# Two-layer decode block on one core: output projection in 512-column products, row quarters summed by an fp32 product, w_down in two loads

## The chip, the core and the metric

One NeuronCore of a Trainium2 chip runs the whole kernel. Its engines each take their own instructions in order: TensorE (PE; its weight loads are shown as PEld), VectorE (DVE), ScalarE (ACT), GpSimd (POOL) and SyncE (SP), which here issues nearly all transfers. Engines wait for one another through semaphores. The metric is the device time of one execution in microseconds, as the median of several runs; a profiled execution gives the trace.

## The reference

Four sequences decode one token each through attention, a gated feed-forward network, the same attention again and the same network again:

```python
x = x + A(_layernorm(x), k_cache, v_cache, wq, wo)
x = x + B(_layernorm(x), w_gate, w_up, w_down)
x = x + A(_layernorm(x), k_cache, v_cache, wq, wo)
x = x + B(_layernorm(x), w_gate, w_up, w_down)

def A(x, k_cache, v_cache, wq, wo):      # B=4, D=512, 32 query heads, 8 kv heads, 4096 keys, head size 128
    q = (x @ wq) as 32 heads; each kv head serves 4 query heads
    p = softmax(q @ k.T * 128 ** -0.5)
    return (p @ v, all 32 heads side by side: 4096 values) @ wo

def B(x, w_gate, w_up, w_down):          # F = 1792
    return (gelu(x @ w_gate) * (x @ w_up)) @ w_down
```

All inputs are bf16. Both layers use the same caches and weights. K and V of one sequence and one kv head are 1 MB each.

## The kernel before

**Staging.** The weights are loaded once and stay: `wq` (4 MB), `wo` in two halves of 2 MB, `wg`, `wu` and `wd` (1.75 MB each). K and V go through `KV`, a tile of 12 slots of 1 MB. The K of a batch element stays in its eight slots for both layers. The V of heads 0 to 6 is loaded a second time for the second layer, that of head 7 is held. So few slots are left to rotate, and a load into a slot waits until the last product that reads it is done. For the last batch element the tile of `wq`, which has no reader any more, gives four more slots. Every load is one instruction on SP's queue (`ld_head` L293, `plain` L650, `ld_wo` L685); SP waits there for the slot, and all later loads wait behind.

**The order of the work.** `Plan` holds every step as a node with an engine, an assumed duration, the steps that it needs, and for TensorE a number of instructions (`ins`). `Plan.run` is a list scheduler: it walks a simulated clock and picks, per engine, the next ready node, with a model of the transfers (`DMA_KB` us per KB and others) and of the fetching of TensorE's instructions in blocks (`BLOCK`, `FIRST_BLOCK`, `FETCH`). Its order is then emitted as it stands, for every engine. The constants thus change only the order. Where it foresees TensorE idle, `spin` (L888) puts in filler matmuls on the identity, whose results nothing reads.

**One batch element `b`, layer `L`.** K heads 5 and 7 are transposed on TensorE (`kturn` L306) and copied back by ACT (`kcopy` L312); the others by DVE in two halves (`turn` L299, node `tn`). Scores of four heads at a time are 32 matmuls (`scores` L348, nodes `sc`), each z in two halves m; then the maximum, the exponent (ACT L371), a transposition on DVE and TensorE (`pswap` L388, in the PSUM tiles T0 and T1; copied by ACT L396), the sums (L401) and the V products: one node `val` per head, 32 matmuls of 128x128 weights (`values` L417). `oscale` (L425, nodes `os`) divides and writes the heads' columns into `OT`.

**The output projection.** `proj` (L547) multiplies each query head's column of `OT` by its 128 rows of `wo`, in four matmuls of 128 columns, each into its own 32-row quarter of the PSUM tile `R0`. The quarter t thus holds output columns 128t to 128t+127. In the first layer the heads are done in three groups as they become ready, `groups` giving (0,1,2,3), (4,5,6), (7); in the second layer all four sequences are projected together at the end of the kernel (`op2`), in four groups. `addback` (L555, L556) transposes the quarters and adds them to `XT`. Then follow the norm (`ln`: L432, L438, L444, L445, L454, ACT L461 and L462), gate and up products (`up` L564), the turn (L571), the GELU in pieces (L587 to L616), `down` (L624, 56 matmuls of 128 columns), `addback` again, the norm and, in the first layer, the query product of the second (`qproj`: L470, ACT L483, DVE L488) and its spreading (`spread_q`: `qs` L527, the replicating product `qp` L537, `qx` L325) ahead of the second layer's scores. The K slots of batch element b are free only after these scores, and so they gate the K loads of b+1. The first V products of the second layer are put between these steps.

**The end.** After the last V load: the remaining V products, `op2`, `addback`, norm, up, GELU, `down`, and the output row (L636, L637, L641), written out by four small transfers (L644).

## Time and profile before

Median of three runs 302.95 us (302.27 to 304.44).

| | |
|---|---|
| profiled execution | 302.36 us |
| its span, first to last instruction | 300.5 us |
| mean granted TensorE clock | 0.949 |
| PE busy | 227.4 us (76%), 4705 matmuls |
| PEld busy | 145.4 us (48%) |
| DVE busy | 132.1 us (44%) |
| ACT busy | 70.0 us (23%) |
| read from HBM | 110.37 MB, 367 GB/s over the span |
| V products L417 | 1920 matmuls on KV, 64.6 us busy |
| projection L547 | 640 matmuls, 14.2 us busy |
| fillers L888 | 181 matmuls |

Busy times of the engines overlap, and a matmul counts as busy for its whole passage through the pipeline, so the 227 us of PE are no measure of what TensorE would need. The idle time of an engine costs only where others wait for it. The chain of waits follows the work that ended last back to what released it; the waits of SP's queue say what each load stood for; "issue" is idle time of an engine in which the profile shows nothing that it waited for.

### The profile page before, as it was taken

The numbers are of one execution on the slowest core, as the hardware profiler recorded it, in microseconds if no ns is written. First come the engines' busy times: TensorE is split into PE (matmuls) and PEld (weight loads), VectorE is DVE, ScalarE is ACT, GpSimd is POOL, SyncE is SP. The second block draws the span as 40 slices with busy tenths as digits, with TensorE's granted clock in tenths as the row PEclk, the third lists the DMA queues.
The fourth block names the chain that finished last, engine by engine and source line by source line (L and its number), as shares of the span: only waits on it lengthen the run. The fifth ranks groups of instructions, "written<-read, shape, count | busy, mean of one in ns | idle before, by whom it ended". The sixth has DMA issues, their size and how long they took to land.

```text
span 300.5 us, 10242 instructions
## 1 busy us (share of the span) xinstructions
PE 227.4 (76%) x4705; PEld 145.4 (48%) x4705; DVE 132.1 (44%) x374; ACT 70.0 (23%) x157; POOL 0.7 (0%) x6
## 2 busy tenths in 40 slices
PE   5987657766778898786868996777577858699694
PEld 1432435432333576554434676553336646457562
DVE  4187702002488642143388730342888205243024
ACT  1020921000021671001215730010247300122000
POOL 0000000000000000000000000000000000000000
PEclk9999999999999799799797997997999999799869
DMA  8999999999949999999999999999999999999600
GB/s 310 409 422 420 366 415 417 399 392 426 416 171 424 421 418 417 416 380 382 366 387 426 418 417 398 373 382 354 374 425 420 413 377 388 368 373 429 266 4 1
DMA packets 18059, 111.02 MB, mean 369 GB/s; under 512 B 1633, under 2 KB 5729, under 8 KB 5729
## 3 DMA queue, kind: packets, MB, share of 16 engines
q1 hardware_dynamic: 17968, 110.37, 91.7%
q8 instruction: 36, 0.59, 0.8%
q14 instruction: 7, 0.05, 0.1%
q10 hardware_dynamic: 48, 0.01, 0.0%
HBM read 110.37 MB, written 0.00 MB: 367 GB/s over the span
## 4 chain that ended last, share of the span: by engine, by line
DMA 53%; PE 24%; SPq 10%; DVE 6%; issue 4%; ACT 3%; DVEq 0%
DMA KV<-in_A_v_cache_dram 34%; DMA KV<-in_A_k_cache_dram 12%; PE O_ps L417 10%; SPq L293 7%; PE S_ps L348 6%; DMA wd_sb<-in_B_w_down_dram 6%; PE R_ps L547 3%; SPq L650 3%; PE R_ps L306 2%; PE R_ps L470 1%; ACT KV L312 1%; DVE KV L299 1%; ACT PA L396 1%; PE R_ps L624 1%; PE T_ps L388 1%
## 5 line engine op out<-in xcount | busy, mean ns | idle before, releaser
L417 PE MATMUL O_ps<-PA,KV 128*128 128x56 bf16 x1920 | 64.6, 191 | 28.6 <-DMA KV<-in_A_v_cache_dram 19.6
L417 PEld LDWEIGHTS <-KV 128*128 128x128 bf16 x1920 | 58.8, 98 | 42.7 <-DMA KV<-in_A_v_cache_dram 30.0
L299 DVE STREAM_TRANSPOSE KV<-KV 128x1024 int32<-128x1024 int32 x48 | 57.0, 1218 | 3.4 <-DMA KV<-in_A_k_cache_dram 3.4
L888 PE MATMUL S_ps<-iden_b 128*128 128x512 bf16 x161 | 42.6, 393 | 3.6 <-DVE iden_b L266 3.6
L348 PE MATMUL S_ps<-KV,PA 128*32 128x512 bf16 x384 | 39.3, 442 | 7.1 <-DVE rdk L407 3.6
L312 ACT ACTIVATE KV<-R_ps 128x512 bf16<-128x512 f32 x64 | 35.1, 596 | 36.2 <-PE R_ps L306 36.2
L888 PEld LDWEIGHTS <-iden_b 128*128 128x128 bf16 x181 | 17.2, 105 | 25.4 <-issue 8.4
L306 PE MATMUL R_ps<-iden_b,KV 128*128 128x128 bf16 x256 | 23.1, 225 | 7.3 <-DMA KV<-in_A_k_cache_dram 3.8
L461 ACT ACTIVATE sm<-sm 128x1 f32<-128x1 f32 (+1 forms) x10 | 2.0, 204 | 102.9 <-DVE sm L454 102.9
L354 DVE TENSOR_REDUCE sm<-S_ps 128x1 f32<-128x512 f32 x16 | 10.8, 674 | 32.6 <-PE S_ps L348 32.6
L306 PEld LDWEIGHTS <-KV 128*128 128x128 bf16 x256 | 16.4, 101 | 15.9 <-issue 8.8
L348 PEld LDWEIGHTS <-PA 128*32 128x32 bf16 x384 | 12.8, 102 | 19.0 <-DVE PA L325 7.2
L547 PE MATMUL R_ps<-wo_sb,OT 128*1 128x128 bf16 (+1 forms) x640 | 14.2, 250 | 5.4 <-DMA wo_sb<-in_A_wo_dram 2.2
L371 ACT ACTIVATE PA<-S_ps,sm 128x512 bf16<-128x512 f32 x16 | 11.7, 732 | 25.9 <-DVE sm L365 11.2
L348 PE MATMUL S_ps<-KV,QN 128*32 128x512 bf16 x128 | 16.4, 381 | 0.0
L547 PEld LDWEIGHTS <-OT 128*1 128x1 bf16 (+1 forms) x640 | 11.4, 96 | 7.8 <-issue 4.3
L425 DVE TENSOR_TENSOR OT<-O_ps,XS 128x12 bf16<-128x12 f32 (+1 forms) x8 | 1.3, 167 | 30.8 <-PE O_ps L417 30.8
L425 DVE TENSOR_TENSOR OT<-O_ps,rdk 128x16 bf16<-128x16 f32 (+3 forms) x17 | 2.9, 170 | 23.4 <-PE O_ps L417 23.3
L470 PE MATMUL R_ps<-wq_sb,xn 128*1 128x512 bf16 (+1 forms) x160 | 11.1, 417 | 1.9 <-DVE xn L445 1.9
L396 ACT ACTIVATE PA<-T_ps 128x512 bf16<-128x512 f32 x16 | 9.5, 595 | 11.1 <-PE T_ps L388 11.1
L571 DVE STREAM_TRANSPOSE PA<-R_ps 128x448 f32<-128x448 f32 x10 | 6.5, 649 | 12.2 <-PE R_ps L564 12.2
L380 DVE STREAM_TRANSPOSE PA<-PA 128x256 int32<-128x256 int32 x16 | 6.9, 432 | 10.0 <-ACT PA L371 10.0
(86 smaller groups left out, 158.5 us busy)
## 6 DMA issues: line engine op xcount, KB each, us to landing
KV<-in_A_v_cache_dram SPq DMA_DIRECT2D x56, 1024.0 KB, 8.9
KV<-in_A_k_cache_dram SPq DMA_DIRECT2D x32, 1024.0 KB, 10.2
wq_sb<-in_A_wq_dram SPq DMA_DIRECT2D x1, 4096.0 KB, 12.3
wo_sb<-in_A_wo_dram SPq DMA_DIRECT2D x2, 2048.0 KB, 24.8
wq_sb<-in_A_v_cache_dram SPq DMA_DIRECT2D x4, 1024.0 KB, 13.0
wg_sb<-in_B_w_gate_dram SPq DMA_DIRECT2D x1, 1792.0 KB
wu_sb<-in_B_w_up_dram SPq DMA_DIRECT2D x1, 1792.0 KB
wd_sb<-in_B_w_down_dram SPq DMA_DIRECT2D x1, 1792.0 KB
```

What stands on the lines that cost most here:

```text
L293: nc.sync.dma_start(out=where[name], in_=src.rearrange("(p c) d -> p (c d)", p=P))
L299: nc.vector.transpose(out=w, in_=w)
L306: nc.tensor.matmul(R_ps[k % 2][:, P * u:P * u + P], lhsT=where[name][:, at:at + P], rhs=iden_b[:], start=True, stop=True)
L312: nc.scalar.activation(out=where[name][:, 512 * k:512 * k + 512], in_=R_ps[k % 2][:], func=ACT.Copy)
L348: nc.tensor.matmul(S_ps[z][32 * t:32 * t + 32], lhsT=w, rhs=k, start=(m == 0 and x == 0), stop=(m == 1 and x == 3))
L354: nc.vector.tensor_reduce(out=cms[:, z:z + 1], in_=S_ps[z][:].rearrange("p c r -> p (c r)"), axis=AX.X, op=ALU.max)
L371: nc.scalar.activation(out=PW[L][z].rearrange("p (a r e) -> p a r e", a=8, e=2), in_=S_ps[z][:].rearrange("p (a e) r -> p a r e", e=2), fu ...
L396: nc.scalar.activation(out=PW[L][z], in_=T_ps[z][:].rearrange("p t x -> p (t x)"), func=ACT.Copy)
L417: nc.tensor.matmul(Ov[L][:, j], lhsT=vw[:, c, :], rhs=w[:, c % 16 // 2, c // 16, :, c % 2].unsqueeze(1).broadcast_to([P, WIDE, 4]), start= ...
L470: nc.tensor.matmul(R_ps[z][32 * jg:32 * jg + nb, :].rearrange("p (h r) -> p h r", h=8), lhsT=xn[:, c, bs], rhs=w[:, z, jg % 2, :, jg // 2, :],
L547: nc.tensor.matmul(R_ps[0][32 * t:32 * t + nb, 0:P], lhsT=src[:, h, b0:b0 + nb], rhs=wo_sb[:, h, P * t:P * t + P], start=(first and h == t ...
L888: nc.tensor.matmul(sinks[place].rearrange("p (a n) -> p a n", a=4), lhsT=iden_b[:], rhs=every, start=True, stop=True)
```

## The change

It does four things.

1. The heads that are ready early (kv heads 0 to 5 in the first layer; 7 and 0 to 5 in the second, by the order of their groups) are projected in one matmul of 512 columns per query head instead of four of 128. The query head's place i within its kv head, not the output column, now chooses the 32-row quarter of `R0`. The four quarters are thus partial sums over all 512 columns. ACT copies 256 columns at a time to SBUF in fp32 (`half_out`), and four fp32 products per half with `pick_b`, which is one in the rows 32i + b, sum the quarters and turn the result at once into T0 (`half_sum`); DVE adds it to `XT` (`add_sums`). Both halves use the same SBUF tile `yq`, so the second copy waits for the first half's products.
2. The heads left (6 and 7 in the first layer, 6 in the second) keep the old form, into `R1` (`proj_last`), and are added by `addback` after the sums.
3. `wd` is loaded in two halves, and `down` is two nodes of 28 matmuls, each waiting for its half.
4. The planner's constants and its model of the instruction fetch are changed (`FETCH`, `FETCH_LAST`, `DMA_KB`, the loads of `wo` at 20.5, the fillers counted in), which gives another order.

```diff
 WIDE = 14
-BLOCK, FIRST_BLOCK, FETCH = 256, 192, 4.6
+BLOCK, FIRST_BLOCK, FETCH, FETCH_LAST = 256, 192, 5.7, 3.9
 HOP = 0.08
 DMA_FIRST = 1.6
-DMA_KB = 0.3095
+DMA_KB = 0.311
 DMA_TAIL = 0.5
...
                 e = s + v["dur"]
+                if v["eng"] == "PE":
+                    gap = min(s - free.get("PE", 0.0), 1.2 if n[0] == "val" else 99.0)
+                    done += 2 * int(max(0.0, FILL * gap - 0.2) / SPIN)
+                    while done > edge:
+                        fetched = max(fetched, s) + (FETCH if s < land or qi < len(self.loads) else FETCH_LAST)
+                        edge += BLOCK
                 while v["ins"] and done + v["ins"] > edge:
...
                     e += max(0.0, fetched - t)
-                    fetched = max(fetched, t) + FETCH
+                    fetched = max(fetched, t) + (FETCH if t < land or qi < len(self.loads) else FETCH_LAST)
                     edge += BLOCK
...
     mask_th = keep([4, 4], FP32, "mask_th")
-    sm = keep([50], FP32, "sm")
+    sm = keep([54], FP32, "sm")
     ones, mask_i, mask_h, rq = sm[:, 0:1], sm[:, 2:6], sm[:, 6:10], sm[:, 10:11]
...
     var = sm[:, 45:49]
+    pick_b = sm[:, 50:54]
     XS = keep([2, CD, B], FP32, "XS")
...
     nc.vector.tensor_copy(out=fold_b[:], in_=fold)
+    nc.vector.tensor_copy(out=pick_b, in_=fold[:, 0:B])
     nc.vector.tensor_reduce(out=mask_h, in_=mask_th[:].rearrange("p t h -> p h t"), axis=AX.X, op=ALU.add)
...
 
-    def proj(src, b0, nb, heads, first, last):
-
+    def proj(src, nb, heads, first, last):
+        def emit():
+            for j in heads:
+                for i in range(4):
+                    nc.tensor.matmul(R_ps[0][32 * i:32 * i + nb, :], lhsT=src[:, 4 * j + i, 0:nb],
+                                     rhs=wo_sb[:, 4 * j + i, :], start=(first and j == heads[0]),
+                                     stop=(last and j == heads[-1]))
+        return emit
+
+    def proj_last(src, nb, heads, first, last):
         def emit():
...
                 for t in range(4):
-                    nc.tensor.matmul(R_ps[0][32 * t:32 * t + nb, 0:P], lhsT=src[:, h, b0:b0 + nb],
+                    nc.tensor.matmul(R_ps[1][32 * t:32 * t + nb, 0:P], lhsT=src[:, h, 0:nb],
                                      rhs=wo_sb[:, h, P * t:P * t + P],
...
 
-    def addback(bs, nb):
+    yq = PD[:, 0:256]
+
+    def half_out(m):
+        def emit():
+            nc.scalar.activation(out=yq, in_=R_ps[0][:, 256 * m:256 * m + 256], func=ACT.Copy)
+        return emit
+
+    def half_sum(m, nb):
+        def emit():
+            for c in range(CD):
+                nc.tensor.matmul(T_ps[0][64 * m:64 * m + 64, 0, nb * c:nb * c + nb],
+                                 lhsT=yq.rearrange("p (x c) -> p c x", c=CD)[:, c], rhs=pick_b[:, 0:nb],
+                                 start=True, stop=True)
+        return emit
+
+    def add_sums(bs, nb):
+        def emit():
+            nc.vector.tensor_tensor(out=XT[:, :, bs], in0=XT[:, :, bs],
+                                    in1=T_ps[0][:, 0, 0:CD * nb].rearrange("p (c b) -> p c b", b=nb), op=ALU.add)
+        return emit
+
+    def addback(bs, nb, z=0):
         def emit():
             yt = PD[:, 0:P].rearrange("p (c x) -> p c x", c=CD)
-            nc.vector.transpose(out=yt, in_=R_ps[0][:, 0:P].rearrange("p (r c) -> p c r", c=CD))
+            nc.vector.transpose(out=yt, in_=R_ps[z][:, 0:P].rearrange("p (r c) -> p c r", c=CD))
             nc.vector.tensor_tensor(out=XT[:, :, bs], in0=XT[:, :, bs], in1=yt[:, :, 0:nb],
...
 
-    def down(nb):
+    def down(nb, k):
         def emit():
             h = ff(nb)[3]
-            for c in range(CF):
+            for c in range(7 * k, 7 * k + 7):
                 for t in range(4):
...
 
+    def ld_wd(k):
+        return lambda pick: nc.sync.dma_start(
+            out=wd_sb[:, 7 * k:7 * k + 7], in_=B_w_down.rearrange("(q c) n -> q c n", q=P)[:, 7 * k:7 * k + 7])
+
     pl.load("x", 0.5, ld_x, None)
...
     loads_k(0)
-    pl.load(("wo", 0), 16, ld_wo(0), None)
+    pl.load(("wo", 0), 20.5, ld_wo(0), None)
     loads_v(0, 0)
-    pl.load(("wo", 1), 16, ld_wo(1), None)
+    pl.load(("wo", 1), 20.5, ld_wo(1), None)
     pl.load("wg", 14, plain(wg_sb[:], B_w_gate, "(q c) n -> q c n"), None)
     pl.load("wu", 14, plain(wu_sb[:], B_w_up, "(q c) n -> q c n"), None)
-    pl.load("wd", 14, plain(wd_sb[:], B_w_down, "(q c) n -> q c n"), None)
+    for k in range(2):
+        pl.load(("wd", k), 7, ld_wd(k), None)
     for b in range(1, B):
...
         if L == 0:
-            return [(0, 1, 2, 3), (4, 5, 6), (7,)]
+            return [(0, 1, 2, 3), (4, 5), (6,), (7,)]
         left = [tuple(j for j in range(4 * z, 4 * z + 4) if j not in HELD[b]) for z in range(2)]
...
         return [(h, [("os", b, 1, i)]) for i, h in enumerate(g)]
+
+    def outproj(tag, b, L, bs, nb, after):
+        pre, p = None, parts(b, L)
+        whole = len(p) - (1 if L else 2)
+        for k, (heads, deps) in enumerate(p[:whole]):
+            pre = add(tag + (k,), "PE", 0.21 * len(heads) + 0.15, deps + [pre] + after,
+                      proj(OT[L], nb, heads, k == 0, k == whole - 1), ins=8 * len(heads))
+        free = [("val", b, 0, j) for j in range(4)]
+        for m in range(2):
+            pre = add(("yo",) + tag + (m,), "ACT", 0.42, [pre] + free, half_out(m), acq=() if m else ("T0",))
+            free = [pre]
+            pre = add(("ys",) + tag + (m,), "PE", 0.5, [pre], half_sum(m, nb), ins=16)
+        xa = add(("ya",) + tag, "DVE", 0.18, [pre], add_sums(bs, nb), rel=("T0",))
+        pre = None
+        for k, (heads, deps) in enumerate(p[whole:]):
+            pre = add(tag + (whole + k,), "PE", 0.21 * len(heads) + 0.15, deps + [pre] + after,
+                      proj_last(OT[L], nb, heads, k == 0, k == len(p) - whole - 1), ins=32 * len(heads))
+        return add(("oa",) + tag, "DVE", 0.52, [pre, xa], addback(bs, nb, 1))
 
...
             if L == 0:
-                pre = None
-                for k, (heads, deps) in enumerate(parts(b, 0)):
-                    pre = add(("op", b, k), "PE", 0.21 * len(heads) + 0.15, deps + [pre, dense_end] + was2,
-                              proj(OT[0], 0, 1, heads, k == 0, k == 2), ins=32 * len(heads))
-                a = add(("oa", b), "DVE", 0.52, [pre], addback(bs, 1))
+                a = outproj(("op", b), b, 0, bs, 1, [dense_end] + was2)
                 a = ln(("f", b), a, bs, 1, rs[:, 0:1])
...
                 add(("zz", b), "DVE", 0.07, [a], clear_sides)
-                a = add(("dn", b), "PE", 0.95, [a, "wd"], down(1), ins=112)
+                for k in range(2):
+                    a = add(("dn", b, k), "PE", 0.48, [a, ("wd", k)], down(1, k), ins=56)
                 a = add(("da", b), "DVE", 0.52, [a], addback(bs, 1))
...
                     add(("val", b, L, j), "PE", 1.03, [name, ("pc", b, L, z)] + prev, values(name, L, j), ins=64)
-                old = [("op", b - 1, m) for m in range(3)] if L == 0 and b else []
+                old = [("op", b - 1, m) for m in range(len(parts(b - 1, 0)))] if L == 0 and b else []
                 add(("os", b, L, i), "DVE", 0.18, [("val", b, L, j) for j in heads] + [("rc", b, L, z)] + old,
...
 
-    a = dense_end
-    last = len(parts(B - 1, 1)) - 1
-    for k, (heads, deps) in enumerate(parts(B - 1, 1)):
-        a = add(("op2", k), "PE", 0.21 * len(heads) + 0.15, deps + [a], proj(OT[1], 0, B, heads, k == 0, k == last), ins=32 * len(heads))
-    a = add("oa2", "DVE", 0.52, [a], addback(al, B))
+    a = outproj(("op2",), B - 1, 1, al, B, [dense_end])
     c = add("rowz", "DVE", 0.1, [("val", B - 1, 1, j) for j in range(8)], rows_clear)
...
     a = add("gc2", "DVE", 0.97, [e, t1], gelu_c(B))
-    a = add("dn2", "PE", 0.95, [a], down(B), ins=112)
+    for k in range(2):
+        a = add(("dn2", k), "PE", 0.48, [a], down(B, k), ins=56)
     add("out", "DVE", 0.3, [a, c], leave)
```

## The prediction

> **What bounds the kernel now.** I read the page's slices first, then stretches of the span, the transfer queue's waits, TensorE in order of time, and the chain of waits. The page:

> ```profile
> DMA  8999999999949999999999999999999999999600
> GB/s 310 409 422 420 366 415 417 399 392 426 416 171 424 421 418 417 416 380 382 366 387 426 418 417 398 373 382 354 374 425 420 413 377 388 368 373 429 266 4 1
> q8 instruction: 36, 0.59, 0.8%
> ```

> The transfers are busy to slice 37 of 40, so the kernel is bound by them, with three exceptions. One: slice 11 falls to 171 GB/s. Two: in three stretches the engines show busy at only 370 to 376 GB/s. Three: after the last load 15 us of compute remain. The 36 instruction packets are 16.4 KB each; 9,410 TensorE instructions (4,705 matmuls and as many weight loads on the page) make 261 to a packet. The stretches (columns: PE, PEld, DVE, ACT, POOL busy, granted clock, DMA share, GB/s):

> ```profile
> 128.00:156.00 28.00, 20.58 (x449) 12.56 (x445) 13.28 (x42) 3.94 (x12) 0.00 (x0) 0.94 0.99 376
> 184.00:220.00 36.00, 27.28 (x603) 17.59 (x598) 17.17 (x51) 3.94 (x12) 0.00 (x0) 0.91 0.98 375
> 244.00:268.00 24.00, 18.12 (x496) 12.39 (x493) 7.87 (x35) 2.40 (x8) 0.00 (x0) 0.93 0.96 370
> 156.00:184.00 28.00, 22.81 (x498) 16.17 (x499) 15.57 (x36) 12.55 (x25) 0.00 (x0) 0.94 1.01 419
> ```

> Against 419 GB/s the first three lose 28 x 43/419 + 36 x 44/419 + 24 x 49/419 = 2.9 + 3.8 + 2.8 = 9.5 us. They are where second-layer V loads rotate through three slots. The queue's waits say what holds the next load there, and TensorE's timeline what holds that:

> ```profile
> SPq L293 <- PE O_ps L417: 40.0, 27, 3.4
> 117.15 0.34 PE L547 MATMUL R_ps<-wo_sb,OT 128*1 128x128 bf16 x11 [0.91 <-issue]
> 129.27 0.39 PE L438 MATMUL R_ps<-XS,sm 128*128 128x8 f32 x2 [0.82 <-issue]
> 183.05 1.52 PE L417 MATMUL O_ps<-PA,KV 128*128 128x56 bf16 x50 [2.38 <-issue]
> 258.85 0.98 PE L417 MATMUL O_ps<-PA,KV 128*128 128x56 bf16 x30 [1.30 <-issue]
> ```

> "issue" breaks a V product or a projection in its middle, where nothing is waited for, some 256 instructions apart: TensorE has run out of fetched instructions. With the smaller ones in the same view (0.41, 0.47; 0.88, 0.15) they make 2.6, 2.4 and 2.3 us around the three stretches, 7.3 in all.

> **Part 1, wd in two loads and the plan's order at 79 us (slice 11).** From the chain of waits:

> ```profile
> 60.84 18.21 DMA wd_sb<-in_B_w_down_dram
> 79.10 0.98 PE R_ps L624 x56
> ...
> 83.92 0.26 DVE qs L527
> 84.18 1.15 DVE KV L299
> 85.33 0.32 DVE PA L325
> 85.65 0.04 issue
> 85.70 2.05 PE S_ps L348 x30
> ```

> The K slots come free after these scores, and the stretch 86:88 moves nothing. Only half of the 56 matmuls still waits for the second load: -0.49. In the new order the K turn of L299 stands behind the query spread of L325; that then waits only for its replicating product (0.16 to 0.20, L537) and two hops, so it starts near 84.5 instead of 85.33: -0.85. What is late next is that K turn, and the second score group, behind which four issued loads (10 us at 2.49 us per MB) give cover. Sum -1.3 (0 if both halves land together and the turn is needed at once). The second wd issue costs SP 0.43 us ahead of batch 1's K loads; three loads queued then hide it.

> **Part 2, fewer instructions.** Per batch six heads change from 96 matmuls of 128 columns to 24 of 512: 192 - 48 = 144 instructions less; eight fp32 products add 32 (two loads and two passes each, as L438 shows): -112, and -136 at the end, where seven heads change. With ten fillers fewer: 4 x 112 + 136 + 20 = 604, 8,806 left. The matmul time itself does not change: 64 of 128 columns take 1.06 us at 177.19 (16.6 ns), 16 of 512 columns 1.06 us at 81.73 (66 ns, L470), so 96 and 24 both make 1.59.

> Counted along the instruction order, 256 instructions take 5.4 to 6.2 us in the stalled runs (111.8, 117.2, 123.4, 129.3), 22 ns each; 112 less is 2.5 us, which covers each batch's 2.3 to 2.6 of stall. I take the 7.3 as gone. Kept ends: none goes (the stalls only move), all goes.

> **Part 3, what is added.** ACT copies of 128x256: between L597's 128x56 (0.25) and L396's 128x512 (0.60), so 0.41, ten of them; ACT is 23% busy. The fp32 group of four products waits for its copy, and behind it on TensorE stand the last head's matmuls and the next V product, for which SP's next load waits. No row shows it. From above: four pairs like L401's (0.30 for two loads of 128 columns) and a pass, 1.31. From below: half of that for 64 columns, at the 0.10 spacing of those loads, 0.5. I take 0.75, nearer below, as the weights are half as wide. [...]

> From the last V product of the first layer to the next V product the trace has 1.0, 1.9 and 1.5 us (126.4, 186.5, 248.4). After: two groups 1.5, the second copy's uncovered 0.2, 16 or 32 matmuls of 17 ns: 2.1 and 2.3; in batch 3 the first group stands before that product, where TensorE idles for the landing, leaving 1.4. Added: 1.1 + 0.4 - 0.1 = 1.4. Batch 0 has cover: its projection ends at 67.3, the gate weights land at 70.5. DVE's added addition (0.17, L425's size) lies beside later work except at the end. The PSUM tile T0 that the groups fill is next needed by the second layer's transposes, over 10 us later.

> Parts 2 and 3 take 7.3 - 1.4 = 5.9 us of waiting from between V products. How much reaches the landings? Room is 9.5, but a product after a stall finds its V landed and catches up. Between none and all I take three quarters: -4.4.

> **Part 4, the end.** The chain, last load to add-back:

> ```profile
> 282.58 0.61 PE O_ps L417 x16
> 283.18 1.48 issue
> 284.67 0.93 PE O_ps L417 x16
> 285.59 1.81 PE R_ps L547 x48
> 287.40 1.60 PE O_ps L417 x32
> 289.00 1.41 PE R_ps L547 x48
> ```

> This is 7.86 us to 290.44, at a granted clock of 0.50 from 283.7. After, at that clock: V product 1.54; the boundary lies 20 instructions into the same product, but the one before it is crossed about one V product earlier, so 0.7 of the stall is left (0 to 1.48); 24 matmuls of 512 columns at 99 ns (3.16 for 32 at 260.60, clock 0.5) 2.38; V product 1.60; groups at 1.0 each; 16 matmuls 0.47; copy 0.1; addition 0.2. Sum 8.99: +1.1 (from -0.6, no stall and groups of 0.5, to +2.5, the whole stall and groups of 1.3).

> **Sum.** -1.3 - 4.4 + 1.1 = -4.6. The profiled execution took 302.36 (span 300.5 and 1.9 around it), the median is 302.95; its lowest run, 302.27, is as good as the profiled one, so I set the sum on 302.36: **297.8**.

> **Rivals.** *Three slots set the pace.* If a slot's turn (5.5 to 7.7 us from issue to landing in the chain) and not TensorE's stalls keeps the queue shallow, parts 2 and 3 give nothing: -1.3 + 1.1, 302.2. For it: 189.48 took 5.93 with no stall near. Against: 27 waits on the product. Chance 0.18.

> *The fp32 groups hold the V products* (slower). Five exposed groups at three quarters and two at the end: 5.75 us per us of group. The sum is zero at 0.75 + 4.6/5.75 = 1.55 us. At 2.6, the upper bound at half clock, it is +6.0: 308.4. For it: nothing shows 64-column fp32 loads. Chance 0.10.

> *The count of matmuls, not their columns, sets the projection.* Then 24 cost 0.4 instead of 1.59: 3 x 1.2 x 0.75 and 1.6 at the end come off: 293.5. L470's 66 ns speaks against it; 0.03. [...]

> *More half clock.* 3.41 us with TensorE busy 1.53 to 1.75 are followed by 0.50 (256.38, 140.32, 280.27); with fewer fillers and stalls moved, two more such pieces on the paced stretches cost 1.3 each (a V product 1.60 for 1.04): 300.4. Chance 0.05, within 1%. [...]

> **Numbers.** The forecast's own case (295 to 299.9) has 0.58; all of the 5.9 passing on with the best end (302.36 - 1.3 - 5.9 - 0.6 = 294.6) 0.06. About 1% is what a measurement here can tell. Faster by over 1%, under 299.9: 0.58 + 0.06 + 0.03 = 0.67; within: 0.18 + 0.05 = 0.23; slower: 0.10. To leave out no more than two in ten the range takes in the three-slot case, a little more for the clock, and the full passing-on with groups at 0.5 in the middle (5 x 0.25 x 0.5 less): 294.0 to 302.8.

> **What would show it.** 34 or 35 instruction packets; the K issue at 87.8 near 86.4; "issue" on TensorE under 2 us between 100 and 262; the three stretches over 390 GB/s; fp32 groups at 0.6 to 0.9; last V landing near 277, then 15 to 17 us. I am wrong if the stretches stay at 375 without stalls, or if a group takes over 1.5.

## The result, and the profile after

The changed kernel takes 313.26 us (median of four runs, 311.6 to 315.63) against 302.61 us for the kernel before in the same comparison (300.64 to 304.44): a ratio of 1.036, 95% interval 1.027 to 1.045, so 10.7 us slower. The prediction was 297.8 us. Medians here and below are over all executions, and ratios over those in the faster of two states that executions fall into, so the two can differ by some tenths of a per cent. The profiled execution took 313.09 us, its span is 311.3 us, and TensorE's mean granted clock fell from 0.949 to 0.901.

The page of after, the rows that answer to those of before:

```profile
PEclk9999999859599999979976999697979995999778
DMA  8999999999905999989999999899999999799600
GB/s 333 389 428 416 364 417 418 380 420 408 378 7 204 427 416 418 418 343 387 362 414 422 416 406 386 319 404 375 359 422 415 409 407 375 288 425 420 259 2 1
q8 instruction: 34, 0.56, 0.7%
```

Counted from 0 as in the prediction, slice 11 moves 7 GB/s and slice 12 moves 204, where before slice 11 alone stood out with 171. It is the stretch from 86 to 98 us, from the first sequence's `down` to its scores of the second layer. The instruction packets are down from 36 to 34, as the change of form should make them. The clock row shows, in tenths, where TensorE was held at half clock for the whole or a part of a slice.

What TensorE did ahead of it, in its timeline (start, duration, line, operation, in brackets what ended the idle time before it):

```profile
66.25 0.60 PE L563 MATMUL R_ps<-wo_sb,OT 128*1 128x128 bf16 x16 [7.49 <-DMA wo_sb<-in_A_wo_dram]
...
67.18 1.70 PE L425 MATMUL O_ps<-PA,KV 128*128 128x56 bf16 x32
69.13 0.60 PE L563 MATMUL R_ps<-wo_sb,OT 128*1 128x128 bf16 x16 [0.26 <-DVE OT L433]
69.66 3.61 PE L942 MATMUL S_ps<-iden_b 128*128 128x512 bf16 x14
73.20 0.60 PE L553 MATMUL R_ps<-wo_sb,OT 128*1 128x512 bf16 x8
...
74.30 1.11 PE L578 MATMUL T_ps<-sm,PA 128*64 128x1 f32 x8 [0.17 <-ACT PA L572]
...
79.00 1.66 PE L601 MATMUL R_ps<-wg_sb,xn 128*1 128x448 bf16 x16 [0.46 <-DVE sm L461]
80.59 3.88 PE L942 MATMUL S_ps<-iden_b 128*128 128x512 bf16 x9
84.40 0.93 PE L601 MATMUL R_ps<-wu_sb,xn 128*1 128x448 bf16 x16
```

The first L563 is the projection of head 6. It waits 7.49 us for the second half of `wo`, and the V product of head 7, whose V landed at 60.2, stands behind it and ends at 68.88 instead of 61.37. Then come 14 fillers of 3.61 us, the two fp32 groups, and 9 more fillers of 3.88 us. Both bursts run after the loads for which their places were to wait have landed: the second half of `wo` at 66.2, the up weights at about 74.8, where they released the up product of the kernel before. The chain of waits of after runs through the same places (start, duration, what):

```profile
51.68 14.53 DMA wo_sb<-in_A_wo_dram
...
69.73 3.54 PE S_ps L942 x14
...
80.66 3.81 PE S_ps L942 x9
...
93.66 2.16 PE S_ps L356 x26
```

The second layer's first scores, which free the K slots, end at 95.7, before at 87.75. The K issue behind them goes out at 95.73 instead of 87.76: 8.0 us of the 10.8 by which the span has grown.

The paced stretches of after, shifted with the work (columns as in the prediction, the last three: granted clock, DMA share, GB/s):

```profile
134.00:164.00 30.00, 23.38 (x489) 15.18 (x488) 13.43 (x45) 4.11 (x12) 0.00 (x0) 0.86 0.96 375
194.00:228.00 34.00, 26.59 (x542) 18.31 (x541) 15.37 (x50) 4.32 (x13) 0.00 (x0) 0.84 0.96 370
252.00:276.00 24.00, 21.59 (x512) 15.57 (x508) 8.67 (x37) 3.17 (x10) 0.00 (x0) 0.86 0.91 359
```

They are no faster than the 376, 375 and 370 of before, at a clock of 0.84 to 0.86 instead of 0.91 to 0.94. Yet the stalls are gone: the rows of "issue" among TensorE's waits between 100 and 262 us made 7.7 us before, and after there is one (total, times, longest):

```profile
PE O_ps L425 <- issue: 1.0, 2, 0.8
```

The transfer queue waits for V products all the same, in the whole span, and more than the 40.0 us of before:

```profile
SPq L301 <- PE O_ps L425: 47.4, 30, 4.6
```

The end, TensorE in order of time:

```profile
292.18 1.53 PE L425 MATMUL O_ps<-PA,KV 128*128 128x56 bf16 x32 [1.45 <-DMA KV<-in_A_v_cache_dram]
293.65 2.52 PE L553 MATMUL R_ps<-wo_sb,OT 128*4 128x512 bf16 x24
...
297.07 1.12 PE L578 MATMUL T_ps<-sm,PA 128*64 128x4 f32 x8
...
298.72 1.12 PE L578 MATMUL T_ps<-sm,PA 128*64 128x4 f32 x8 [0.21 <-ACT PA L572]
...
301.88 1.67 PE L601 MATMUL R_ps<-wg_sb,xn 128*4 128x448 bf16 x16
```

From this V product to the norm it takes 8.57 us, as before (8.66). But the gate product takes 1.67 us where before it took 0.93: half clock follows the two fp32 groups, and from the norm to the end of the kernel it takes 10.55 us instead of 9.24.

**Where the half clock comes from.** In the traces of before and after, a granted clock of 0.50 comes in pieces of 3.41 us, or multiples. By the mean clock there are 2 x (1 - 0.949) x 300.5 = 30.7 us of it before and, worked out in the same way, 61.6 us after. Two windows of after that lie on the grid of these pieces, and the one behind each (length, then the engines' busy times with PE's first, then granted clock, DMA share, GB/s):

```profile
131.98:135.40 3.42, 3.15 (x63) 2.90 (x63) 0.16 (x1) 0.38 (x1) 0.00 (x0) 1.00 1.00 410
135.40:138.81 3.41, 3.41 (x64) 3.40 (x64) 1.29 (x8) 0.30 (x2) 0.00 (x0) 0.50 0.78 300
193.42:196.84 3.42, 3.26 (x78) 3.03 (x78) 0.16 (x1) 0.39 (x2) 0.00 (x0) 1.00 1.03 422
196.84:200.25 3.41, 2.54 (x38) 2.36 (x38) 0.82 (x5) 0.00 (x0) 0.00 (x0) 0.50 0.75 310
```

TensorE shows as busy for 3.15 and 3.26 of 3.42 us, and half clock follows all the same. The two windows for line 578 alone, the fp32 groups:

```profile
131.98:135.40 3.42, 1.85 (x15) 1.77 (x15) 1.00 1.00 410
193.42:196.84 3.42, 1.76 (x14) 1.68 (x14) 1.00 1.03 422
```

Without the groups 1.30 and 1.50 us are left (1.43 and 1.66 if the time that the groups share with their neighbours stays in). At 1.53 to 1.75 the kernel before went to half clock. The reading, which needs a test (below): in what sets the granted clock, a product of one column, or of four, does not count as work, whatever its record says.

### The profile page after: what moved, and what is told of

Same layout as the page of the kernel before. It is cut to its first block, busy times and chain, and to the rows that moved or that the text cites. A ratio compares the mean times of both kernels' runs of the same rounds, so it can differ in the third digit from the quotient of the medians.

```text
span 311.3 us, 9656 instructions
## 1 busy us (share of the span) xinstructions
PE 246.1 (79%) x4403; PEld 152.9 (49%) x4403; DVE 132.9 (43%) x384; ACT 73.7 (24%) x167; POOL 0.7 (0%) x6
## 4 chain that ended last, share of the span: by engine, by line
DMA 47%; PE 34%; SPq 6%; ACT 5%; DVE 4%; issue 2%; ACTq 0%
DMA KV<-in_A_v_cache_dram 30%; DMA KV<-in_A_k_cache_dram 12%; PE O_ps L425 11%; SPq L301 6%; PE S_ps L356 6%; DMA wo_sb<-in_A_wo_dram 5%; PE S_ps L942 4%; PE R_ps L601 4%; PE T_ps L578 2%; ACT KV L320 2%; PE R_ps L314 1%; PE R_ps L553 1%; ACT PA L379 1%; PE R_ps L661 1%; ACT PA L404 1%
## 5 line engine op out<-in xcount | busy, mean ns | idle before, releaser
L425 PE MATMUL O_ps<-PA,KV 128*128 128x56 bf16 x1920 | 66.9, 193 | 20.8 <-DMA KV<-in_A_v_cache_dram 17.8
L425 PEld LDWEIGHTS <-KV 128*128 128x128 bf16 x1920 | 61.1, 100 | 36.1 <-DMA KV<-in_A_v_cache_dram 27.6
L942 PE MATMUL S_ps<-iden_b 128*128 128x512 bf16 x152 | 46.2, 438 | 3.6 <-DVE iden_b L273 3.6
L362 DVE TENSOR_REDUCE sm<-S_ps 128x1 f32<-128x512 f32 x16 | 10.8, 675 | 29.1 <-PE S_ps L356 28.7
L314 PEld LDWEIGHTS <-KV 128*128 128x128 bf16 x256 | 15.7, 98 | 13.8 <-issue 9.8
L356 PEld LDWEIGHTS <-PA 128*32 128x32 bf16 x384 | 12.9, 101 | 17.2 <-DVE PA L333 8.1
L572 ACT ACTIVATE PA<-R_ps 128x256 f32<-128x256 f32 x10 | 3.8, 384 | 60.8 <-PE R_ps L553 50.8
L433 DVE TENSOR_TENSOR OT<-O_ps,XS 128x4 bf16<-128x4 f32 (+1 forms) x12 | 1.8, 162 | 38.3 <-PE O_ps L425 38.3
L356 PE MATMUL S_ps<-KV,QN 128*32 128x512 bf16 x128 | 18.1, 412 | 0.0
L578 PE MATMUL T_ps<-sm,PA 128*64 128x1 f32 (+1 forms) x80 | 11.2, 261 | 0.8 <-ACT PA L572 0.8
L578 PEld LDWEIGHTS T_ps<-sm,PA 128*64 128x64 f32 x80 | 10.3, 214 | 2.2 <-ACT PA L572 1.9
L478 PE MATMUL R_ps<-wq_sb,xn 128*1 128x512 bf16 (+1 forms) x160 | 9.8, 378 | 1.9 <-DVE xn L453 0.9
```

The source lines that it names most:

```text
L314: nc.tensor.matmul(R_ps[k % 2][:, P * u:P * u + P], lhsT=where[name][:, at:at + P], rhs=iden_b[:], start=True, stop=True)
L356: nc.tensor.matmul(S_ps[z][32 * t:32 * t + 32], lhsT=w, rhs=k, start=(m == 0 and x == 0), stop=(m == 1 and x == 3))
L362: nc.vector.tensor_reduce(out=cms[:, z:z + 1], in_=S_ps[z][:].rearrange("p c r -> p (c r)"), axis=AX.X, op=ALU.max)
L425: nc.tensor.matmul(Ov[L][:, j], lhsT=vw[:, c, :], rhs=w[:, c % 16 // 2, c // 16, :, c % 2].unsqueeze(1).broadcast_to([P, WIDE, 4]), start= ...
L578: nc.tensor.matmul(T_ps[0][64 * m:64 * m + 64, 0, nb * c:nb * c + nb], lhsT=yq.rearrange("p (x c) -> p c x", c=CD)[:, c], rhs=pick_b[:, 0:nb],
L942: nc.tensor.matmul(sinks[place].rearrange("p (a n) -> p a n", a=4), lhsT=iden_b[:], rhs=every, start=True, stop=True)
```

## The experiments

Ratios are to the kernel before, run beside them on the same chip (302.5, 301.2 and 302.1 us in the three sets). The theories' letters belong to their set: the first set is the lost need, the need taken from the kernel before, and the first two kernels with `wd`; the second is the kernel without fillers, the bf16 sums and the two with the old constants; the third is the rest. Half clock is worked out as above.

**The lost need.** The groups of the first layer were three; `parts` gives the need of a half of `wo` to the groups 0 and 1. With four groups, those of heads 6 and 7 have none, and they begin a chain of their own (`pre = None`), so the planner may put them ahead of the load. The edit gives it back to all groups from the second on:

```diff
-            return [(h, [("os", b, 0, i)] + ([("wo", i)] if i < 2 else [])) for i, h in enumerate(g)]
+            return [(h, [("os", b, 0, i)] + ([("wo", min(i, 1))])) for i, h in enumerate(g)]
```

> Theory A (the planner no longer knows that heads 6 and 7 of batch 0 need the second half of wo; TensorE stands 7.5 us in front of a V product and the dense path of batch 0 runs 8 us late): with that need written in, head 6's products follow the V product of head 7 again, the first K load of batch 1 is issued at 86 to 88.5 us instead of 95.7, and the time is 303 to 306 us. Rival B (the 512-column form with its fp32 groups and the lower clock costs the time all along): the K issue moves by under 3 us and the time stays at 309 us or above.

306.01 us, ratio 1.010 (1.004 to 1.016), so 2.6% or 7.9 us of the loss are gone. The V product of head 7 is back at 60.28, and the chain has the scores behind the wait for `wo` where they were before:

```profile
51.67 14.44 DMA wo_sb<-in_A_wo_dram
66.15 0.63 PE R_ps L553 x8
...
71.94 1.66 PE R_ps L601 x16
...
85.71 2.13 PE S_ps L356 x24
```

The K issue is at 87.75. The gate product, at 71.94, still begins 1.4 us later than in the kernel before, behind the two fp32 groups. The kernel is slower than before by 1%, so a second cause was left.

**The same need taken from the kernel before** (`if i < 2` becomes `if i < 1`), old form, old constants:

> The kernel before with one thing taken from the planner: that the group of heads 4 to 6 of batch 0 needs the second half of wo. The old 128-column form, the old constants, one load of wd. Theory A: TensorE stands 7 to 8 us at 58.8 us with the V product of head 7 behind it, the K issue at 87.8 moves to 92 to 97, and the time is 307 to 312 us. Rival B: the wait is made up before the weights of the network land; the time stays within 302 to 304.5 us.

303.74 us, ratio 0.999 (0.992 to 1.006). The wait is there, and it costs next to nothing in the end:

```profile
66.38 1.45 PE L547 MATMUL R_ps<-wo_sb,OT 128*1 128x128 bf16 x48 [7.69 <-DMA wo_sb<-in_A_wo_dram]
67.76 1.67 PE L417 MATMUL O_ps<-PA,KV 128*128 128x56 bf16 x32
...
71.33 4.48 PE L888 MATMUL S_ps<-iden_b 128*128 128x512 bf16 x20
```

The scores end at 90.62, 2.9 us late and not 8.0, and the time has not grown, so Theory A falls. The wait by itself isn't the 8 us; something behind it is.

**The fillers behind it.** The changed kernel, its need not mended, without the two bursts of 14 and 9 fillers:

```diff
-            if name in gaps:
+            if name in gaps and name not in (("op", 0, 1), ("up", 0, 1)):
```

> The changed kernel as it is, need not mended, without two bursts of fillers of the first sequence: the 14 ahead of the projection's second group and the 9 ahead of the second half of the up product (23 of 171 fillers; their results are read by nothing). Theory D: the wait for the second half of wo costs only some 3 us at the K issue (as in the old form with the need taken away), and the other 5 us are these fillers, planned for an idle time that is already spent, 3.6 and 3.9 us in the trace. Then the K issue after the second layer's first scores is at 88 to 89.5 instead of 95.7 and the median is 305 to 308. Rival E: the wait sets it, and without the fillers TensorE only waits longer or stays longer at half clock: K issue at 93 or later, median 311 or more.

304.56 us, ratio 1.014 (1.010 to 1.018): 2.2% or 6.6 us less, and a little under the 305 to 308 expected. The wait of 7.5 us is unchanged, and the up product follows the gate product at once (77.15 instead of 84.40):

```profile
66.18 0.60 PE L563 MATMUL R_ps<-wo_sb,OT 128*1 128x128 bf16 x16 [7.50 <-DMA wo_sb<-in_A_wo_dram]
...
75.70 1.66 PE L601 MATMUL R_ps<-wg_sb,xn 128*1 128x448 bf16 x16 [0.46 <-DVE xn L453]
77.15 1.66 PE L601 MATMUL R_ps<-wu_sb,xn 128*1 128x448 bf16 x16
```

The K issue is at 89.22, as the fillers' theory had it; the rival, that the wait sets it, falls. A filler is work like any other once it is in the queue: these 23 were planned into an idle time that on the chip had been spent earlier, at the wait which the plan did not know.

**wd in two loads alone**, first with the old constants, then with the new ones, both in the old form:

```diff
-    pl.load("wd", 14, plain(wd_sb[:], B_w_down, "(q c) n -> q c n"), None)
+    for k in range(2):
+        pl.load(("wd", k), 7, ld_wd(k), None)
...
```

> The kernel before with wd in two loads alone. Part 1 of the prediction: half of the down products no longer waits and the K turn stands behind the query spread, the K issue at 87.8 comes at 86.2 to 86.9, and the time falls by 0.8 to 1.5 us. Rival: both halves land together or the gain is lost later; less than 0.5 us either way.

> The kernel before with wd in two loads and the new constants and fetch model of the planner; the projection is the old one. Theory A (new order and constants do no harm by themselves): 299 to 303.5 us, K issue at 86 to 87.5. Rival C (the new constants give an order that is worse for the loads, whatever the projection): over 305 us with the K issue on time.

299.37 us, ratio 0.987 (0.977 to 0.996), and 301.42 us, ratio 0.999 (0.995 to 1.003). In both, the scores that free the K slots end at 87.2 instead of 87.75. The first rests on four executions and was run again:

> The kernel before with wd in two loads alone, again, in five rounds beside the run above, since its first ratio (0.987) rests on four executions. Part 1 of the prediction (-1.3 us): 0.994 to 0.998. As read from the first run: 0.985 to 0.990. Against the run above it says what the new form at the end alone is worth: 2 us by the traces (0.007), nothing if the end's clock evens out.

299.57 us, ratio 0.991 (0.988 to 0.995). So part 1 is a gain, of 2.6 us (1.6 to 3.6), more than the 1.3 expected. Only 0.5 us of it is seen on the path that the prediction named. With the new constants, which the changed kernel has, no gain is left: in that trace "issue" on TensorE between 100 and 262 us makes 9.5 us, against 4.4 and 4.6 in the two traces with the old ones.

**The fp32 groups.** The kernel with the mended need and its order unchanged, with the partial sums copied and added in bf16:

```diff
-    yq = PD[:, 0:256]
+    yq = PA[:, 1024:1280]
...
-                                 lhsT=yq.rearrange("p (x c) -> p c x", c=CD)[:, c], rhs=pick_b[:, 0:nb],
+                                 lhsT=yq.rearrange("p (x c) -> p c x", c=CD)[:, c], rhs=fold_b[:, 0:nb],
```

> The kernel with the mended need (median 306.0), its order unchanged, with the row quarters summed in bf16 instead of fp32: ACT writes the 256 columns as bf16 and the four products per half read bf16 (rounding of the partial sums is coarser, nothing else changes). Theory A: the fp32 groups are what makes the 512-column form slow between the V products: 1.12 us each, two per sequence, and TensorE counts as nearly idle in them, so that the half clock which follows stays on for the V products behind them (10.2 us of half clock at 123 and at 188 in that run, against 3.4 with the old projection). Then a group takes 0.3 to 0.5 us, the half clock after it is down to 3.4 us, and the median is 299 to 302. Theory B: the three slots of the rotating V loads set the pace, whatever stands between the products: groups shorter as above, but the median within 1 us of 306, and the last V landing within 1 us of 288.7.

297.3 us, ratio 0.983 (0.978 to 0.988), against 1.010 with fp32: 2.7% or 8.1 us, more than was expected. A group takes 0.40 us instead of 1.12, which for ten groups is 7.2 us, two of them beside the wait for `wg`. The mean granted clock over all executions rises from 0.923 to 0.943. The profiled ones have 68.5 and 37.9 us of half clock, but that of the mended need is the slowest of its kernel, at 0.888. At the end the gate product is back at full clock:

```profile
284.57 0.40 PE L578 MATMUL T_ps<-fold_b,PA 128*64 128x4 bf16 x4
284.90 0.39 PE L563 MATMUL R_ps<-wo_sb,OT 128*4 128x128 bf16 x16
285.50 0.40 PE L578 MATMUL T_ps<-fold_b,PA 128*64 128x4 bf16 x4 [0.21 <-ACT PA L572]
...
287.72 0.93 PE L601 MATMUL R_ps<-wg_sb,xn 128*4 128x448 bf16 x16 [0.28 <-DVE xn L453]
```

From the last V landing to the end (by the transfers' records) it takes 12.9 us. With fp32 it is 17.1 us in the changed kernel, 17.2 with the need mended and 17.2 without the fillers. In the middle, which is the stretch before it, from the landing of the V of head 7 of sequence 1 to the last V landing, these three take 163.8, 166.5 and 161.3 us, against 161.1 with the bf16 sums. So about half of the 8.1 us lies at the end, where nothing covers the groups; what they cost in the middle differs from trace to trace.

**Length or clock?** Two kernels with the bf16 sums in which the time of a group is drawn out again, once with the same narrow products, once with wide ones. The first issues the four products three times:

```diff
-            for c in range(CD):
+            for c in range(3 * CD):
+                c = c % CD
```

> The kernel with the bf16 sums, its order unchanged, each group of four products issued three times, so that a group takes 1.1 to 1.2 us as the fp32 one did (0.40 with one). The result is the same, the third pass writes what the first wrote. Theory F (what the fp32 groups cost is their duration and that products of one column leave TensorE idle for the clock gate: windows of 3.41 us with such a pair in them go on at half clock although the records show 3 us of work): the loss of the fp32 form comes back almost whole, ratio to the kernel before 1.000 to 1.012, half clock 60 us or more. Theory G (something else in the fp32 products, not their length): ratio 0.985 to 0.993.

The second puts fillers of 384 columns behind each group:

```diff
+            for _ in range(4):
+                nc.tensor.matmul(T_ps[0][:, 1:4, :], lhsT=iden_b[:],
+                                 rhs=iden_b[:].unsqueeze(1).broadcast_to([P, 3, P]), start=True, stop=True)
```

> The kernel with the bf16 sums, each group followed by four fillers of 384 columns (some 0.7 us at full clock, results read by nothing), so that the time until the next V product is that of the tripled group, but full of wide products. Theory F: fewer windows at half clock than with the tripled group by 10 us or more (near or under the 40 us of the bf16 sums), and 2 to 5 us faster than the tripled group: ratio 0.988 to 1.000. Pure duration, without the clock: the same as the tripled group within 1 us.

Tripled: 300.82 us, ratio 1.000 (0.996 to 1.003), half clock 45.2 us. With fillers: 298.37 us, ratio 0.989 (0.985 to 0.994), half clock 17.2 us. In all twelve executions of the first the mean granted clock lies between 0.919 and 0.960, in all six of the second between 0.970 and 0.981. A tripled group took 0.88 us and not the 1.1 expected, a group with fillers 1.15, so the faster of the two has the longer group. The same place in both, as windows on the grid; first the tripled groups, then the fillers:

```profile
188.14:191.55 3.41, 3.41 (x93) 3.14 (x90) 0.88 (x5) 0.38 (x1) 0.00 (x0) 1.00 0.92 384
191.55:194.97 3.42, 3.42 (x54) 2.13 (x54) 0.58 (x5) 0.41 (x2) 0.00 (x0) 0.50 0.84 278
```

```profile
184.93:188.35 3.42, 3.42 (x81) 2.57 (x80) 0.74 (x5) 0.38 (x1) 0.00 (x0) 1.00 1.02 422
188.35:191.76 3.41, 2.80 (x71) 1.95 (x68) 1.51 (x7) 0.41 (x2) 0.00 (x0) 1.00 0.93 322
```

By the records TensorE is busy without a gap in both first windows, yet half clock follows only the one with the two tripled groups in it (2 x 0.88 us of its 3.41). So in this pair the one-column products are what went as idle time. The two kernels lie 3.1 us apart, in spite of the longer groups of the faster, which length alone cannot explain. The 60 us of half clock that Theory F expected of the tripled groups were not reached: their mean clock over all executions is 0.937, hardly under the 0.943 of the short groups, and the 1.7% that they lose against these (1.000 against 0.983, in two sets) is about their added length, ten times 0.48 us. How the 8.1 us of the fp32 form split between length and clock these runs don't say. The fillers add 0.75 us to each of ten groups and cost only 1.9 us (0.989 against 0.983, again in two sets); that the higher clock makes up for the rest is likely but not shown by itself.

**The constants.** The mended kernel with the constants and the fetch model of before, in fp32 and in bf16:

> The kernel with the mended need and all of the new form, planned with the constants and the fetch model of the kernel before. Theory A (fp32 groups): the groups are still there, so 305 to 307. Theory C (the new constants are a part of the loss, as 301.4 against 299.4 with the old projection hints): 302.5 to 304.5.

> The bf16 sums and the old constants together, with the mended need. Theory A and C together: 297 to 299.5, the fastest of all so far. A alone: 299 to 302, as with the bf16 sums and the new constants. Theory B (pace set by the slots, the form worth nothing either way): 303 to 306. The prediction's own part 2 (fewer instructions give 4.4 us once the price of the groups is gone) would have 295 to 297.

306.13 us, ratio 1.018 (1.012 to 1.024), and 297.49 us, ratio 0.984 (0.979 to 0.989). Against the new constants, 1.010 and 0.983. So no gain of the old constants is seen in the new form, and the theory that the new ones are a part of the loss is not borne out, although it looked like it in the old form (0.999 against 0.987 and 0.991). It rests on the bf16 pair: the fp32 one has the widest spread of all, from 300.42 us at a mean clock of 0.943 to 309.79 at 0.900, and its ratio says little beside 1.010. The execution that was profiled is its fastest; its trace, with 161.3 us in the middle and 15.1 from the last landing to the end, isn't built on here.

**What the new form is worth.** The new form (bf16) at the end alone, the first layer in the old form, wd in two loads, old constants:

> The kernel before with wd in two loads and with the new form (bf16 sums) in the second layer's projection alone, at the end of the kernel; the first layer's four projections have the old form, the constants are the old ones. Theory H (the rival that three slots set the pace: between the V products the new form gains nothing even with cheap sums, what it gains it gains after the last landing, 12.9 us from there to the end against 15.1): the same time as the bf16 form with old constants everywhere, ratio 0.980 to 0.987, last V landing at 282 to 284 as with wd in two loads alone. The prediction's part 2 (fewer instructions in the middle give several us): 2 us or more slower than that form everywhere, ratio 0.990 or more.

298.88 us, ratio 0.989 (0.986 to 0.993), between the two expectations. Against wd in two loads alone (0.991, same comparison) the new form at the end gives nothing that could be measured. Against the new form everywhere (0.984, another comparison) it lacks 0.5%, and the intervals overlap. The traces do not show that half per cent: the middle takes 160.5 and 160.9 us in the old form with wd in two loads (two profiled executions), 161.1 and 161.7 in the new form with bf16 sums. Whether the form gains 1.6 us in the middle or nothing stays open.

The fastest kernel is that with the mended need and bf16 sums, 0.983 of the time before. That this is close to what the prediction had for the changed kernel (297.8 of 302.36, or 0.985) is luck: its part 1 gave more than was forecast, and its part 2 next to nothing. Its partial sums are rounded to bf16 before they are added, which the fp32 form avoids.

## Why the prediction was wrong, step by step

Of the 15.5 us between forecast and result, 7.9 are the lost need with the fillers behind it, and most of 4.4 is a gain from the stalls that did not come. The rest, an estimate of 3 to 4 us, is the price of the groups above what the sum had, less whatever part 1 gave beyond its 1.3.

**Batch 0 has cover** is the step that failed first, in part 3: "Batch 0 has cover: its projection ends at 67.3, the gate weights land at 70.5." It priced the added operations and took the order for granted. In the order that the planner makes, head 6's projection stands ahead of head 7's V product with a wait for `wo` that the plan doesn't know. The projection's wide part ended not at 67.3 but at 73.8, then came the fp32 groups, and the gate product began at 79.0 instead of 70.5. Removing the fillers gave back 6.6 us, mending the need 7.9. Part 1 did read the new order, at 84 us; at 60 it was not read, and half clock, the groups and the fillers in that place were all taken as hidden. Even with the need mended the cover is too short: the gate product then begins at 71.94.

**A group at 0.75 us** (part 3): 1.12, inside the kept bounds of 0.5 to 1.31. The four products appear as eight matmuls of 0.26 us. The copies, 0.41, were 0.38. The middle's terms add up to 2.0 and 2.2 where it writes 2.1 and 2.3, which changes nothing here.

**The price of a group was its length alone.** That is the second failed step. By the prediction's own price, 5.75 us per us of group, the 0.72 us between an fp32 and a bf16 group would be worth 4.1 us; 8.1 were measured. Two things are missing in it: batch 0's groups, which had no cover after all, and the clock. "More half clock" was a rival with a chance of 0.05, as two pieces that fall at random. In the changed kernel half clock follows each of the five pairs of groups, within two windows of 3.41 us. The rival "the fp32 groups hold the V products" had the sign right (306.0 with the need mended lies between the forecast and its 308.4), but it asked for groups of 1.55 us or more, as it let the gain of the stalls stand; without that gain, and with the clock, 1.12 were enough.

**Three quarters of the stalls reach the landings** (parts 2 and 3, -4.4). The stalls went as said: 1.0 us of issue left between 100 and 262, none with the bf16 sums (0.2 with the old constants), 4.4 with wd in two loads alone. But of the 4.4 us in the middle little came: it takes 162.2 us in the kernel before, 161.1 and 161.7 without stalls (bf16 sums), and 160.5 and 160.9 with 4.4 and 4.6 us of them. This fits the rival "three slots set the pace", up to the open 1.6 us; no run changes the number of slots, so that the slots are the cause is not shown. One trace speaks against it: wd in two loads with the new constants has 9.5 us of stalls and takes 164.5 us there, but its order is another too. The argument against the rival, the queue's 27 waits on V products, was no argument: with the stalls gone there are 30 such waits and 47.4 us instead of 40.0, and with the bf16 sums 27 and 40.4.

**Part 1** was right in sign and too small: -2.6 against -1.3 with the old constants, of which only 0.5 us came by the path that it named; where the rest comes from the runs don't show. The K issue at 86.4 was not reached by wd alone (87.2), but with the new order and bf16 sums it was at 86.7.

**Part 4**, the end, +1.1: most terms held (24 matmuls of 512 columns 2.45 us to the next product against 2.38, groups 1.12 against 1.0). But the 0.7 of stall was gone, and the second V product took 1.03 instead of 1.60, as the clock was back at full by then; so the stretch up to the norm came out at -0.1, in part by luck of the clock. And the sum stopped there, while half clock behind the groups lengthened what follows by 1.3. At full clock both forms take the same from the last landing to the end: 12.9 us in the new one with bf16 sums, 13.1 and 13.2 in the old one in two executions whose end was at full clock.

## What to carry to other kernels

When a group of work is split, look for what its index carried: here a wait for a load hung on the place in a list, and the planner, freed of it, put a blocked instruction ahead of a ready one. Fillers planned for an idle time turn into pure cost when that time is spent elsewhere, so read them as work on the path whenever an order changes. And price a TensorE operation by two numbers, its length and the columns that it moves: in the changed kernel half clock followed each of the five pairs of groups, whose products have one column or four, and what stands behind them paid, as the gate product at the end with 1.67 us instead of 0.93.
